# A fused linear attention and gated feed-forward kernel: batch 1's convolution moved wholly to VectorE, convolution buffers cut into one-batch units, and a new written-out order

## The chip, the cores and the metric

The kernel runs on one core of a Trainium2 chip. The metric is the device time of one launch in microseconds. A core has TensorE (matrix products, written to PSUM banks), VectorE, ScalarE and GpSimd (elementwise work), and SyncE. In the profile they are PE (PEld for its weight loads), DVE, ACT, POOL and SP. DMAs are issued by SP and POOL (and two by ACT at the start); POOL's are queue q0, SP's are q1 in the profile.

## What is computed

Eight batches, eight heads, 576 positions, head size 64, model width 512, inner width 1024, in float32; inside the kernel the operands of matrix products are bfloat16.

```python
kv = np.einsum('bhsd,bhse->bhde', k, v)
out = np.einsum('bhsd,bhde->bhse', q, kv)
rms = np.sqrt(np.mean(out * out, axis=-1, keepdims=True) + 1e-06)
x = out / rms * g_norm          # then heads are put side by side: (B, S, 512)
h = np.maximum(x @ w_in, 0.0)   # (B, S, 1024)
# conv_out: three taps along the positions, zero-padded, a weight per channel
for k in range(3):
    conv_out += conv_w[k] * hp[:, k:k + S, :]
gate = 1.0 / (1.0 + np.exp(-conv_out))
return h * gate @ w_out         # (B, S, 512)
```

## The kernel before

The kernel is a list of small operations (the functions marked `@op`) and a string, `ORDER` (L67), that is its schedule. Each token names an operation with its arguments, `@` and the buffer slots that it takes, and `:1` where the work goes to the other of VectorE and ScalarE than by default. The loop at L797 calls them in that order, and each engine then runs its own instructions in the order in which they were recorded; a dependency added at the end (L807 on) keeps it so. So `ORDER` sets the order on TensorE, VectorE, ScalarE and on both DMA queues at once. Waits between engines follow from the data and from the slots: an operation that takes a slot waits until its last user is done.

The stages of a batch b (t counts the four pairs of heads, u the two halves of them, f the eight 128-wide tiles of the inner width, e the two halves of 288 positions):

- `Lq`, `Lk`, `Lv` (L301): loads of q, k and v on POOL's queue, 576 KB each in bfloat16, into two slots for each of the three. Batch 0 comes in smaller pieces (`pre`), and batch 1 in halves. `Li` and `Lo` load the weights w_in and w_out, on the same queue.
- `kv` (L358): k times v for all pairs of heads, 12 matmuls of 96x64 tiles for each pair. `kvc` and `kvn` copy the result to SBUF; `ky` (on ScalarE or VectorE) or `kx` (a DMA on SP, L449) make the copy `kvx` with the halves exchanged.
- q has to be transposed. Batches 0 to 4 do it on TensorE (`qt0`, `qt`, L380 and L388) and copy it out (`qc0`, `qc`). Batches 5, 6 and 7 do it by DMA (`dq`, L436): two transposes each on SP's queue, from the loaded q to a slot of `qT`.
- `ot` (L430, L431) or `oq` (L464, 64x64 tiles, for batches 4 to 7): q times kv. `sq` squares it on ScalarE, `oc` copies it to SBUF.
- The norm: `on`/`nl`/`mu0` in batches 0 and 1; from batch 2 `ss` (L575) adds the squares in 128x32 tiles, `ln` takes the root, `sl` splits it in two, `sp` (L603) spreads it over the partitions in 32x128 tiles, and `mu` multiplies it in. Batch 7's factor goes through DRAM (`fw`, `fr`, L610 to L617).
- `hm` (L640; `ha`, `hb` are its halves): eight matmuls of 128x288 for the inner activation of one f. `re` is the relu that writes h.
- The convolution runs in groups c (`CONV`: group 0 is batch 0, 1 is batch 1, and 2, 3 and 4 are two batches each), for pairs j of f. On VectorE: `ta` (L699, L700; two multiplications for one f), `aa` (L706; their shifted sum) and `ab` (L712; adds the middle tap). On TensorE: `cm` (L731; six matmuls with a diagonal matrix). `sg` (L742, L745) is the sigmoid on ScalarE, `mg` (L751) multiplies it into h. Before the change f 6 and 7 of group 0 and of group 1 go by `cm`, everything else by VectorE.
- `om` (L761) multiplies with w_out, eight matmuls of 128x512 for 128 rows of a pair p of batches (in p 0 and 3 in two halves of four). `oh` (L776) does the last row tile in two halves. `ea`/`eh` copy the result out, `st`/`sh` (L795, L790) store it by DMA on SP's queue.

The convolution's buffers are two tiles, `taps0` and `taps1`, of shape [128, 2 taps, 2 f, 2 batches, 584] (L198); a one-batch group uses half of one. TensorE's matmuls use the whole 128x128 array or a part of it, its tile (the profile writes it before the moving operand's shape, as 64*64). `unread` (L427) issues matmuls whose result nobody reads.

Of the kernel before, what the change touches and what calls it, by code (L numbers as in the profile page):

```python
# [52 lines left out]
BF16 = mybir.dt.bfloat16  # L53
# [22 lines left out]
sq.1.0@4 re.0.1 qt.1.1@4 hm.0.0@2 on.1.0@6 mg.0.3 qc.1.1@3 ot.1.1@4 nl.1.0@4 re.0.0:1 sq.1.1@5 kv.1.2.2@2
kvc.1.2.2.0 ta.0.0@1 mu0.1.0 kvc.1.2.2.1 on.1.1@6 Li.2 ot.1.2@2 nl.1.1@5 ot.1.3@0 ta.0.1 sq.1.2@6 mu0.1.1 aa.0.0
unread.1@6 on.1.2@6 sq.1.3@7 ab.0.0 nl.1.2@6 mu0.1.2 on.1.3@4 nl.1.3@7 Lk.2.0@0 qt.2.0@6 sg.0.3 qt.2.1@4 mu0.1.3
ha.1.2@2 hb.1.2 qc.2.1@4 sg.0.2 qc.2.0@0 ha.1.3@0 hb.1.3 re.1.2 re.1.3 hm.1.7@4 Lv.2.0@0 hm.0.4@2 mg.0.1 Lq.3.0@1
hm.0.5@0 sg.0.1 Lk.3.0@1 Lv.3.0@1 re.1.7 sg.0.0 pl ta.1.2@0 re.0.4 ta.1.3 re.0.5 hm.1.4@4 kv.2.0.4@2 Lo.0 aa.1.1  # L80
ab.1.1 mg.0.0 sg.1.3 sg.1.2 kvc.2.0.4.0@0 hm.1.5@0 kvc.2.0.4.1 ta.0.4@1 ta.0.5 ot.2.0@2 mg.1.1 aa.0.2 hm.1.6@6
re.1.4 ot.2.2@4 re.1.5 sq.2.0@0 ta.1.4@0 ab.0.2 re.1.6 qt.3.1@0 oc.2.0:1@0 qt.3.0@6 qc.3.1@1 hm.1.1@2 ot.2.1@0
sq.2.2@1 sg.0.4 oc.2.2@1 sg.0.5 sq.2.1@2 Lo.1 Lq.4.0@0 Lq.5.0@1 qc.3.0@2 ta.1.5 ot.2.3@4 re.1.1:1 sq.2.3@3 hm.1.0@6
oc.2.1 Lk.4.0@0 Lv.4.0@0 kv.3.0.4@2 re.1.0 ss.2@3 oc.2.3 mg.0.2 ln.8@0 aa.1.2 kvc.3.0.4.0:1@1 kvc.3.0.4.1:1 ab.1.2
unread.3@0 ot.3.0@4 ta.1.0@1 ot.3.1@6 sq.3.0@4 ot.3.2@0 ta.1.1 al.x2@0 oc.3.0@2 aa.1.0 sq.3.2@5 oc.3.2@3 sq.3.1@6
om.0.3.0@2 om.0.0.0@3 oc.3.1 sl.8@0 om.0.1.0@4 ot.3.3@0 om.0.1.4 ab.1.0 om.0.3.4 sq.3.3@7 oc.3.3 sp.2.1@6,0 ss.3@5
dq.5.0@3 ea.0.1@0 mu.2.1.0 Lk.5.0@1 mu.2.1.1 om.0.0.4 ea.0.3@1 ln.1@0 sp.2.0@4,6 mu.2.0.1 mu.2.0.0 dq.5.1@0
om.0.2.0@2 Lv.5.0@1 sg.1.5 sg.1.4 qtp.4.0@0 cm.1.6@6 qc.4.0@4 mg.1.2 ea.0.0@2 hm.2.5@4 sl.1@0 hm.2.2@0 sg.1.1
om.0.2.4 re.2.5 sg.1.6@0 re.2.2 ea.0.2@3 sg.1.0 sp.3.0@6,4 cm.1.7@0 mu.3.0.1 mu.3.0.0 hm.2.4@2 hm.2.7@6 sg.1.7
sp.3.1@0,4 mg.1.0 re.2.4 mg.1.3 kv.4.0.4@2 mu.3.1.0 mu.3.1.1 re.2.7 kvn.4.0.4 ky.4.0.4.0 ky.4.0.4.1 qtp.4.1@6  # L90
hm.3.4@0 hm.3.5@4 re.3.4 oq.4.1@0 re.3.5 qc.4.1@2 ta.2.4@1 ta.2.5 oq.4.0@2 hm.2.6@6 sq.4.0@0 hm.3.3@4 oc.4.0@1
hm.3.6@2 sq.4.1@1 re.2.6 aa.2.2 Lq.7.0@0 hm.3.7@6 re.3.3 oc.4.1 hm.3.1@0 re.3.6 re.3.7 hm.3.2@6 hm.2.3@2 om.0.6.0@4
st.0.0 ab.2.2 ta.2.6@0 sg.2.5 re.3.1 re.3.2 ta.2.7 oq.4.3@6 oq.4.2@0 sg.2.4 re.2.3 kv.5.0.4@5 sq.4.2@2 Lv.7.0@0
Lk.7.0@0 om.0.6.4 om.0.5.0@2 aa.2.3 ab.2.3 Lk.6.0@1 Lv.6.0@1 kvn.5.0.4 sq.4.3@3 oc.4.2@0 mg.2.2 ky.5.0.4.0:1
ea.0.6@4 ss.4@3 dq.7.0@1 oc.4.3 ky.5.0.4.1:1 oq.5.0@0 oq.5.1@4 sq.5.0@4 ta.2.2@1 om.0.5.4 sq.5.1@5 oc.5.0:1@2
om.0.4.0@6 oc.5.1 ta.2.3 oq.5.3@0 oq.5.2@4 aa.2.1 om.0.8.0@7 ea.0.5@5 ab.2.1 sq.5.3@6 om.0.4.4 sq.5.2@7 ss.5 ln.2@0
om.0.8.4 hm.2.1@2 oc.5.2@3 ea.0.8@6 oc.5.3 re.2.1 sl.2@0 hm.2.0@4 sp.4.1@0,2 ea.0.4@7 om.0.7.0@7 re.2.0 mu.4.1.0
mu.4.1.1 sp.4.0@4,0 kv.7.0.4@6 mu.4.0.0 sg.2.2 mu.4.0.1 om.0.7.4 kvn.7.0.4:1 sg.2.3 ea.0.7@2 sp.5.0@4,2 hm.3.0@0
al.h2@1 re.3.0 kx.7.0.4.0 dq.7.1@4 mu.5.0.1 mu.5.0.0 hm.4.5@2 re.4.5 sp.5.1@6,4 hm.4.1@0 mg.2.1 mu.5.1.0 hm.4.2@2
mu.5.1.1 ta.2.0@1 sg.2.7 hm.4.0@6 hm.5.3@4 ta.2.1 re.4.1 sg.2.6 mg.2.3 kx.7.0.4.1 re.4.0 re.4.2 oq.7.0@0 re.5.3  # L100
kv.6.0.4@6 oq.7.1@4 sq.7.0@0 hm.5.2@2 oc.7.0@1 aa.2.0 Lq.6.0@1 hm.4.3@0 st.0.4 dq.6.0@2 sq.7.1@1 oc.7.1 re.5.2
hm.4.4@4 st.0.5 kvn.6.0.4:1 ab.2.0 ta.3.2@0 re.4.3 hm.5.6@0 st.0.1 ta.3.3 hm.5.4@2 hm.5.1@6 sg.2.1 sg.2.0 re.4.4
re.5.6 re.5.1 re.5.4 hm.5.0@4 oq.7.3@6 oq.7.2@0 aa.3.1 re.5.0 mg.2.0 om.1.6.0@2 om.1.3.0@3 ab.3.1 st.0.3 kx.6.0.4.0
st.0.6 ta.3.0@1 dq.6.1@3 sq.7.3@2 sq.7.2@3 ta.3.1 sg.3.3 sg.3.2 hm.5.5@4 oc.7.2@0 st.0.7 aa.3.0 ss.7@0 mg.3.1 ln.4@0
al.x3@1 ab.3.0 ta.3.4@0 ea.1.3@7 re.5.5 om.1.1.0@1 oc.7.3 ea.1.6@5 kx.6.0.4.1 om.1.0.0@0 fw.4 fr.7.0@0 ea.1.1@0
oq.6.0@2 oq.6.2@6 oq.6.3@4 om.1.8.0@1 ta.3.5 ea.1.0@1 sq.6.2@4 fr.7.1@1 oc.6.2@2 oq.6.1@6 aa.3.2 om.1.4.0@0 sq.6.0@5
sq.6.3@6 sq.6.1@7 oc.6.0@3 ss.6@2 ab.3.2 oc.6.1 ea.1.8@4 ln.3@0 ea.1.4@2 hm.4.6@6 om.1.5.0@2 oc.6.3 sl.3@0 st.1.0
mu.7.0.0 sp.6.0@4,0 mu.7.0.1 re.4.6 sg.3.5 sg.3.4 ea.1.5@1 mu.6.0.0 mu.6.0.1 om.1.2.0@6 hm.4.7@4 hm.5.7@0 mu.7.1.0
om.1.7.0@7 re.4.7 sg.3.1 re.5.7 st.0.8 sp.6.1@4,2 st.0.2 st.1.8 mg.3.2 mu.7.1.1 al.h3@0 ta.3.6@0 ea.1.2@6 ea.1.7@3
hm.7.6@0 ta.3.7 sg.3.0 hm.7.2@6 re.7.6 re.7.2 mu.6.1.0 mu.6.1.1 aa.3.3 mg.3.0 ab.3.3 hm.6.0@4 re.6.0 hm.7.1@0  # L110
hm.7.0@4 re.7.1 re.7.0 st.1.2 hm.6.1@0 hm.7.3@4 hm.6.2@6 hm.7.5@2 re.6.1 ta.4.0@1 st.1.1 st.1.7 sg.3.6 sg.3.7 ta.4.1
# [13 lines left out]
def kernel(  # L125
# [11 lines left out]
    nc = tc.nc  # L137
# [708 lines left out]
```

## Time and profile before

| what | us |
|---|---|
| median of 3 runs | 180.41 (179.9 to 182.42) |
| span of the profiled execution, first to last instruction | 177.6 |
| TensorE busy | 168.4 |
| ScalarE busy | 149.7 |
| VectorE busy | 139.5 |
| GpSimd busy | 30.8 |

The profiled execution is one of its own; its span leaves out what lies around the first and last instruction, so it is set beside the lowest of the runs, 179.9, and the median. TensorE's granted clock is 1.00 in every stretch. Matmuls overlap, so a duration of a matmul (286 ns for 128x288) is longer than its share of TensorE's time; the chain, which runs from start to start, gives the share.

### The profile page before, as it was taken

The page shows a single profiled execution, that of the slowest core. Times are in us where ns is not written, and L with a number is a line of the kernel's source. Part 1 is how long each engine was busy: PE and PEld are TensorE (multiplying, and loading weights), DVE is VectorE, ACT ScalarE, POOL GpSimd, SP SyncE. Part 2 cuts the span into 40 slices and gives each one's busy share as a digit, 9 for nine tenths or more (in the row PEclk, how much of TensorE's full clock was granted, in tenths as well). Part 3 has the DMA queues.
Part 4 walks back from the last instruction along what each step waited for, and adds up shares of the span by engine and source line. Part 5 has one row for each costly group of instructions (what it writes and reads, how often), then busy time and mean ns, then how long its engine had stood idle before and what let it go on. Part 6 is the DMA issues. An engine that isn't in the chain of part 4 may idle for free.

```text
span 177.6 us, 4060 instructions
## 1 busy us (share of the span) xinstructions
PE 168.4 (95%) x1641; PEld 101.3 (57%) x1660; DVE 139.5 (79%) x235; ACT 149.7 (84%) x233; POOL 30.8 (17%) x54
## 2 busy tenths in 40 slices
PE   6989996999999999999999999999999999999992
PEld 2545753877545677753667764444677764444541
DVE  5665669999998898999799999939999999950000
ACT  2479899999999969999999999999989987764332
POOL 7995516402600013050000000000000000000000
PEclk9999999999999999999999999999999999999999
DMA  6999999999999999999999950197040003422696
GB/s 155 188 183 197 200 204 201 205 203 206 205 204 203 198 192 139 174 203 198 160 201 179 293 128 0 53 219 263 21 160 0 4 0 143 152 82 99 258 352 219
DMA packets 36219, 29.49 MB, mean 166 GB/s; under 512 B 8528, under 2 KB 31720, under 8 KB 36200
## 3 DMA queue, kind: packets, MB, share of 16 engines
q0 software_dynamic: 21760, 15.96, 59.5%
q1 hardware_dynamic: 14400, 13.26, 28.9%
q8 instruction: 13, 0.21, 0.4%
q14 instruction: 6, 0.05, 0.1%
q10 hardware_dynamic: 40, 0.01, 0.0%
HBM read 33.70 MB, written 9.58 MB: 244 GB/s over the span
## 4 chain that ended last, share of the span: by engine, by line
PE 70%; DMA 20%; POOL 4%; ACT 2%; issue 2%; POOLq 0%; ACTq 0%
PE bank L761 33%; PE bank L640 27%; DMA v_sb<-in_v_dram 10%; DMA k_sb<-in_k_dram 7%; DMA q_sb<-in_q_dram 4%; PE bank L358 3%; PE bank L464 2%; POOL q_sb L241 1%; PE bank L603 1%; PE bank L575 1%; POOL v_sb L241 1%; POOL k_sb L241 1%; PE bank L776 1%; PE bank L731 1%; PE bank L388 1%
## 5 line engine op out<-in xcount | busy, mean ns | idle before, releaser
L640 PE MATMUL bank<-xT,w_in_sb 128*128 128x288 bf16 x496 | 64.5, 286 | 0.1
L761 PE MATMUL bank<-w_out_sb,h 128*128 128x512 bf16 x268 | 63.0, 379 | 1.1 <-issue 0.6
L640 PEld LDWEIGHTS <-w_in_sb 128*128 128x128 bf16 x496 | 47.6, 98 | 14.1 <-issue 0.5
L761 PEld LDWEIGHTS <-h 128*128 128x128 bf16 x280 | 26.3, 98 | 30.6 <-issue 1.9
L646 ACT ACTIVATE h<-bank 128x576 bf16<-128x576 f32 x61 | 37.9, 657 | 4.2 <-PE bank L640 3.9
L745 ACT ACTIVATE taps<-taps,cwn 128x1152 bf16<-128x1152 bf16 (+1 forms) x36 | 38.2, 1094 | 0.1
L341 ACT ACTIVATE row<-bank 128x512 f32<-128x512 f32 (+1 forms) x37 | 21.3, 598 | 12.3 <-PE bank L761 9.3
L751 DVE TENSOR_TENSOR h<-h,taps 128x2304 bf16<-128x2304 bf16 (+1 forms) x20 | 22.2, 1113 | 2.0 <-ACT taps L745 1.2
L706 DVE TENSOR_TENSOR taps<-taps 128x2304 bf16<-128x2304 bf16 (+1 forms) x18 | 20.9, 1160 | 0.4
L712 DVE TENSOR_TENSOR taps<-taps,h 128x2304 bf16<-128x2304 bf16 (+1 forms) x18 | 20.8, 1153 | 0.3
L699 DVE TENSOR_SCALAR taps<-h,cwn 128x1152 bf16<-128x1152 bf16 (+1 forms) x36 | 16.7, 463 | 2.5 <-ACT h L646 2.4
L493 ACT ACTIVATE sq<-bank 128x576 bf16<-128x576 f32 x28 | 17.9, 676 | 0.0
L700 DVE TENSOR_SCALAR taps<-h,cwn 128x1152 bf16<-128x1152 bf16 (+1 forms) x36 | 17.5, 487 | 0.0
L629 DVE SCALAR_TENSOR_TENSOR xT<-o,cw,bank 128x576 bf16<-128x576 f32 x20 | 15.3, 809 | 2.7 <-PE bank L603 2.5
L341 ACT ACTIVATE o<-bank 128x576 f32<-128x576 f32 x22 | 15.0, 694 | 0.0
L213 ACT ACT_TABLE_LOAD x10 | 12.8, 1283 | 2.5 <-issue 2.4
L301 POOL DMA_DIRECT2D q_sb<-in_q_dram x8 | 6.2, 772 | 31.4 <-PE bank L388 16.6
L427 PE MATMUL bank<-fill 128*128 128x512 bf16 x25 | 9.0, 480 | 1.7 <-DVE fill L228 1.5
L358 PEld LDWEIGHTS <-k_sb 96*64 96x64 bf16 x384 | 7.3, 114 | 4.0 <-issue 2.6
L358 PE MATMUL bank<-v_sb,k_sb 96*64 96x64 bf16 x384 | 8.5, 199 | 1.0 <-DMA k_sb<-in_k_dram 0.7
L301 POOL DMA_DIRECT2D k_sb<-in_k_dram x8 | 6.1, 758 | 14.4 <-PE bank L358 12.5
L562 DVE SCALAR_TENSOR_TENSOR xT<-bank,cw,root 128x576 bf16<-128x576 f32 x7 | 5.6, 815 | 1.8 <-ACT root L542 1.7
(93 smaller groups left out, 135.3 us busy)
## 6 DMA issues: line engine op xcount, KB each, us to landing
out_dram<-row SPq DMA_DIRECT2D x35, 256.0 KB, 2.8
q_sb<-in_q_dram POOLq DMA_DIRECT2D x6, 576.0 KB, 13.7
k_sb<-in_k_dram POOLq DMA_DIRECT2D x6, 576.0 KB, 14.7
v_sb<-in_v_dram POOLq DMA_DIRECT2D x6, 576.0 KB, 16.3
factor<-factor SPq DMA_DIRECT2D x4, 288.0 KB, 4.9
w_in_sb<-in_moe_w_in_dram POOLq DMA_DIRECT2D x4, 256.0 KB, 8.7
w_out_sb<-in_moe_w_out_dram POOLq DMA_DIRECT2D x2, 512.0 KB, 18.0
q_sb<-in_q_dram POOLq DMA_DIRECT2D x4, 144.0 KB, 4.6
```

Source lines behind the costliest of these rows:

```text
L341: nc.scalar.activation(to, fr, AX.Copy)
L358: nc.tensor.matmul(ps[i][i * D:(i + 1) * D, t - t0, :], k_sb[:, 2 * t + i, r * D:(r + 1) * D], v_sb[:, 2 * t + i, r * D:(r + 1) * D], star ...
L493: nc.scalar.activation(in_order(b, s), product(b, t), AX.Square)
L640: nc.tensor.matmul(ps[:, e, :HS], w_in_sb[:, t, f * P:(f + 1) * P], x[:, t, e * HS:(e + 1) * HS], start=(t == 0), stop=(t == NT - 1))
L646: nc.scalar.activation(to, fr, AX.Relu)
L699: nc.vector.tensor_scalar_mul(tap[:, 0, f % 2, :n, 8:8 + S], h[:, f], cwn[:, 0, f:f + 1])
L700: nc.vector.tensor_scalar_mul(tap[:, 1, f % 2, :n, :S], h[:, f], cwn[:, 2, f:f + 1])
L706: nc.vector.tensor_add(tap[:, 1, :, :n, :S], tap[:, 0, :, :n, 7:7 + S], tap[:, 1, :, :n, 1:1 + S])
L712: nc.vector.tensor_add(y, y, h[:, 2 * j:2 * j + 2])
L745: nc.scalar.activation(y, y, AX.Sigmoid, scale=cwn[:, 1, f:f + 1])
L751: nc.vector.tensor_mul(h, h, T["tap", c, j][:, 1, :, :n, :S])
L761: nc.tensor.matmul(T["om", p, m], h[:, f, m * P:(m + 1) * P], w_out_sb[:, f, :], start=(f == 0), stop=(f == NF - 1))
```

## The change

Three things change. Batch 1's tiles f 6 and 7 are convolved by VectorE (`ta`, `aa`, `ab`) and no longer by `cm`. The convolution's buffers become one tile of four one-batch units; a two-batch group takes two neighbouring units, seen through a rearranged view, a one-batch group takes one. And `ORDER` is written anew, by a planner that counts each change of TensorE's tile shape. The new order also chooses again which engine runs `re`, `oc`, `ea`, `kvc`, `kvn`, `ky`, `qc0` and `dg`, and the order of the loads on POOL's queue and of the transposes, kvx copies and stores on SP's.

The code outside `ORDER`:

```diff
+    def units(n):
+        s = slots.pop(0)
+        return taps[:, s:s + n].rearrange("p b k f w -> p k f b w")
...
-    taps = [consts.tile([P, 2, 2, 2, TW], BF16, name=f"taps{i}") for i in range(2)]
+    taps = consts.tile([P, 4, 2, 2, TW], BF16, name="taps")
...
-        for t in taps:
-            nc.vector.memset(t[:, 0, :, :, 7:8], 0.0)
-            nc.vector.memset(t[:, 1, :, :, S:S + 1], 0.0)
+        nc.vector.memset(taps[:, :, 0, :, 7:8], 0.0)
+        nc.vector.memset(taps[:, :, 1, :, S:S + 1], 0.0)
...
-            T["tap", c, f // 2] = taps[slots.pop(0)]
+            T["tap", c, f // 2] = units(CONV[c][1])
...
-                T["tap", c, f // 2] = taps[slots.pop(0)]
+                T["tap", c, f // 2] = units(CONV[c][1])
```

Of `ORDER`, lines with the tokens that matter to what follows: batch 1's last pair, the transposes, batch 6's and 7's loads, and the stores and kvx copies around them.

```diff
-dq.5.0@3 ea.0.1@0 mu.2.1.0 Lk.5.0@1 mu.2.1.1 om.0.0.4 ea.0.3@1 ln.1@0 sp.2.0@4,6 mu.2.0.1 mu.2.0.0 dq.5.1@0
-om.0.2.0@2 Lv.5.0@1 sg.1.5 sg.1.4 qtp.4.0@0 cm.1.6@6 qc.4.0@4 mg.1.2 ea.0.0@2 hm.2.5@4 sl.1@0 hm.2.2@0 sg.1.1
-om.0.2.4 re.2.5 sg.1.6@0 re.2.2 ea.0.2@3 sg.1.0 sp.3.0@6,4 cm.1.7@0 mu.3.0.1 mu.3.0.0 hm.2.4@2 hm.2.7@6 sg.1.7
...
-hm.3.6@2 sq.4.1@1 re.2.6 aa.2.2 Lq.7.0@0 hm.3.7@6 re.3.3 oc.4.1 hm.3.1@0 re.3.6 re.3.7 hm.3.2@6 hm.2.3@2 om.0.6.0@4
-st.0.0 ab.2.2 ta.2.6@0 sg.2.5 re.3.1 re.3.2 ta.2.7 oq.4.3@6 oq.4.2@0 sg.2.4 re.2.3 kv.5.0.4@5 sq.4.2@2 Lv.7.0@0
-Lk.7.0@0 om.0.6.4 om.0.5.0@2 aa.2.3 ab.2.3 Lk.6.0@1 Lv.6.0@1 kvn.5.0.4 sq.4.3@3 oc.4.2@0 mg.2.2 ky.5.0.4.0:1
-ea.0.6@4 ss.4@3 dq.7.0@1 oc.4.3 ky.5.0.4.1:1 oq.5.0@0 oq.5.1@4 sq.5.0@4 ta.2.2@1 om.0.5.4 sq.5.1@5 oc.5.0:1@2
...
-al.h2@1 re.3.0 kx.7.0.4.0 dq.7.1@4 mu.5.0.1 mu.5.0.0 hm.4.5@2 re.4.5 sp.5.1@6,4 hm.4.1@0 mg.2.1 mu.5.1.0 hm.4.2@2
-mu.5.1.1 ta.2.0@1 sg.2.7 hm.4.0@6 hm.5.3@4 ta.2.1 re.4.1 sg.2.6 mg.2.3 kx.7.0.4.1 re.4.0 re.4.2 oq.7.0@0 re.5.3
-kv.6.0.4@6 oq.7.1@4 sq.7.0@0 hm.5.2@2 oc.7.0@1 aa.2.0 Lq.6.0@1 hm.4.3@0 st.0.4 dq.6.0@2 sq.7.1@1 oc.7.1 re.5.2
...
+Lq.5.0@1 dq.5.0@2 ea.0.2@3 re.2.2 ab.1.1 hm.2.7@4 re.2.7 ab.1.3 sp.3.0@0,6 sg.1.1 hm.2.4@2 mu.3.0.1 mu.3.0.0
+mg.1.0 hm.2.3@4 sp.3.1@0,6 re.2.4 sg.1.2 kv.4.0.4@2 mu.3.1.0 mu.3.1.1 kvn.4.0.4:1 re.2.3 dq.5.1@0 qtp.4.1@4 qc.4.1@1
...
+ab.2.2 ta.2.6@0 re.3.3 om.0.7.0@0 oq.4.1@6 Lq.7.0@0 sg.2.5 re.3.2:1 sg.2.4 oq.5.2@2 Lq.6.0@1 sq.4.1@3 re.3.1:1
...
+oq.5.0@4 sq.5.0@6 ta.2.2@2 oq.5.1@6 om.0.7.4 oc.5.0@3 om.0.4.0@1 ss.4@3 Lk.7.0@0 dq.6.1@1 sq.5.1@7 ss.5 ln.2@0
...
+ea.0.6@6 sp.4.1@4,2 Lv.7.0@0 mu.4.1.0 mu.4.1.1 dq.7.1@0 om.0.8.4 re.2.1 sg.2.6 sp.4.0@6,4 mu.4.0.0 dq.7.0@2 kv.7.0.4@0
+mu.4.0.1 hm.3.0@2 sp.5.0@6,4 kvn.7.0.4 Lv.6.0@1 re.3.0:1 mu.5.0.1 ea.0.8@7 sg.2.7 st.0.8 mu.5.0.0 al.h2@0 hm.4.0@0
+st.0.6 hm.4.5@2 st.0.5 al.x3@0 re.4.0 re.4.5 kx.7.0.4.0 sp.5.1@0,4 sg.2.2 hm.4.1@6 re.4.1 mu.5.1.0 kx.7.0.4.1 mu.5.1.1
...
+hm.4.4@0 Lk.6.0@1 re.5.4 oq.7.1@2 oq.7.0@4 re.4.4 kv.6.0.4@6 sq.7.0@0 mg.2.1 kvn.6.0.4 sq.7.1@1 dq.6.0@3 hm.5.3@0
```

On SP's queue the order up to batch 7's products thus goes from two transposes of batch 5, a store, a transpose of batch 7, a kvx copy, the other transpose of batch 7 and a kvx copy, to two transposes of batch 5, a store, one of batch 6, two of batch 7, three stores and two kvx copies. The products `oq.7.0` and `oq.7.1` read the transpose `dq.7.0` and both kvx copies. On POOL's queue the loads for batches 6 and 7 go from q7, v7, k7, k6, v6, q6 to q7, q6, k7, v7, v6, k6. The loads ahead of w_out's are the same ones in another order; the last of them is batch 3's q in place of its v. The number of changes of TensorE's tile shape in the order (a tile of more than 64 rows or columns counted as full in that direction) goes from 80 to 73.

## The prediction, made before the changed kernel ran

> **What bounds the kernel now.** I read the page first, for who is busy, then the chain in order of time, for where the end comes from.
>
> ```profile
> span 177.6 us, 4060 instructions
> PE 168.4 (95%) x1641; PEld 101.3 (57%) x1660; DVE 139.5 (79%) x235; ACT 149.7 (84%) x233; POOL 30.8 (17%) x54
> PE 70%; DMA 20%; POOL 4%; ACT 2%; issue 2%; POOLq 0%; ACTq 0%
> ```
>
> Three engines are close to full. The chain runs over loads first (DMA 20%) and over TensorE after that. Its pieces (start, us, what):
>
> ```profile
> 28.67 17.11 DMA v_sb<-in_v_dram
> 45.78 0.14 issue
> 45.91 0.95 PE bank L358 x48
> ...
> 57.05 0.74 PE bank L731 x6
> ...
> 79.40 1.83 PE bank L761 x8
> ...
> 96.64 0.25 PE bank L464 x4
> ...
> 119.65 1.73 PE bank L761 x8
> ```
>
> Until 45.78 the load queue decides: v of batch 3 lands there, 17.11 us after its issue, because everything ahead in that queue has to land first. From 45.9 to 174.3 nearly every piece is TensorE with no gap, so whatever leaves TensorE there leaves the time. Six L731 matmuls take 0.74 us, 0.123 each. Eight L761 matmuls take 1.73 us where the next group has the same tile shape and 1.83 where it has another (at 79.40 a 64-row group follows): a change of tile shape costs 0.1 us.
>
> Next the busy time by stretch (start:end, length, then PE, PEld, DVE, ACT, POOL), to see who stands close behind TensorE:
>
> ```profile
> 50.00:60.00 10.00, 9.78 (x76) 5.27 (x75) 8.70 (x16) 9.97 (x18) 0.00 (x0) 1.00 1.32 204
> 60.00:70.00 10.00, 10.00 (x136) 7.20 (x135) 8.25 (x13) 8.00 (x15) 2.29 (x3) 1.00 1.32 175
> 70.00:80.00 10.00, 9.79 (x125) 6.19 (x126) 9.67 (x13) 10.00 (x18) 2.45 (x3) 1.00 1.30 183
> 80.00:100.00 20.00, 19.68 (x241) 12.41 (x242) 18.94 (x27) 19.94 (x30) 0.00 (x0) 1.00 1.28 197
> ```
>
> VectorE is 91% busy from 50 to 100 (45.56 of 50) and ScalarE 96%. The last column is GB/s: about 200, flat, so DMA is saturated there too. That made me look at the queues: SP's instructions and the landing times of the transposes (L436), then POOL's loads.
>
> ```profile
> 56.40 7.41 SPq L436 DMA_TRANSPOSE qT<-q_sb  x2
> 78.24 1.51 SPq L436 DMA_TRANSPOSE qT<-q_sb  x1
> 90.41 0.56 SPq L449 DMA_DIRECT2D kvx<-kvn  x1
> ```
>
> ```profile
> DMA to landing us min/median/max: 4.2/10.7/16.0
> ```
>
> ```profile
> 65.74 0.77 POOL L301 DMA_DIRECT2D q_sb<-in_q_dram  x1 [16.55 <-PE bank L388]
> 66.50 0.77 POOL L301 DMA_DIRECT2D v_sb<-in_v_dram  x1
> 67.26 0.77 POOL L301 DMA_DIRECT2D k_sb<-in_k_dram  x1
> ```
>
> A transpose lands 4.2 to 16.0 us after its issue, at best when no load runs beside it. The three loads at 65.74 are batch 7's; batch 6's k, v and q go last, from 77.14.
>
> **The change, part by part.** The sum is made on the profiled execution, 177.6 us. The median of the runs, 180.41, lies 2.8 above that span; I add 2.8 at the end.
>
> Batch 1's last pair of tiles. Off TensorE: cm.1.6 and cm.1.7, 12 matmuls at 0.123 = 1.5 us, on the path: **-1.5**. On VectorE: four multiplications (0.28 to 0.36 each), aa (0.76) and ab (0.75), 2.7 to 3.0 us. ScalarE's two sigmoids read SBUF (0.78) in place of PSUM (0.65): +0.3.
>
> Tile shapes. Counting groups in the two orders, with rows over 64 as a full tile, shape changes fall from 80 to 73, and behind the first output matmul from 49 to 45: 4 x 0.1 = **-0.4**. The other three, and two fewer filler matmuls, lie ahead of 45.8, where loads decide: 0.
>
> First output matmul. It needs w_out, whose loads stand behind the same loads as before. I take 0; bounds -0.6 (it started at 48.56, the last v landed at 45.78 and half of w_out, 0.52 MB at 204 GB/s, takes 2.6) and +1.0 (batch 3's q is now last, so transposes, two copies of 0.75 and products follow it).
>
> Moved evictions and the one-batch units. Net seven relus, five o copies and nine row copies go from ScalarE to VectorE, and some kv copies go back. At 0.67, 0.67 and 0.6, with the convolution's 2.7, less about 2 going back: VectorE +14 us, ScalarE -9. Some 3.3 of it are evictions after 160, where VectorE was idle. Ahead of that VectorE's work nears 99% of TensorE's. The cover of the moved work is TensorE's own stream, and that cover is now as thin as the difference, about 1 us. Bounds: 0, and +9 if VectorE keeps the roughly 10 us of waits that it has from 50 to 160. I take 0, as the next item gives VectorE time to catch up. Two-batch buffers become two strided pieces with the same element counts; no row shows such a shape. The nearest, 2x576 pieces, take 0.76 for 1152 and 1.36 for 2304 elements. I take 0; bounds 0 and, if a split cost as much as two instructions (2 x 0.76 against 1.36), 0.16 on each of the 36 long additions and products, 5.8, inside the +9.
>
> Queues. This is what I expect to decide. POOL's order was q7, v7, k7, k6, v6, q6; it becomes q7, q6, k7, v7, v6, k6. q6 takes the slot of batch 5's q and so waits until both transposes of batch 5 have landed; k7 and v7 now stand behind it. SP's order becomes batch 6's first transpose, then batch 7's two, then three output stores, then batch 7's kvx copies; the first product of batch 7, which was ready with room to spare, needs the third transpose and the copies. Step by step, with 0.59 MB a load, 2.9 us at 204 GB/s:
> v of the third batch lands at 45.8 as now (q of it, after the change); w_out adds 5.2 and five loads (v4, k4, q4, v5, q5) 14.5: q5 lands at 65.4, where now it lands before 56.40, when its transpose goes out.
> Its two transposes took 17.9 us now (56.40 to 58.3 + 16.0), with loads running all along. Only k5 and q7 are left to run beside them, to about 72. Bounds 73.8 (two at 4.2) and 83.3; I take 76.
> q6 goes out then. A load into an empty queue took 4.1 for a quarter of the size at the start, so about 6.3: q6 lands at 82.3, and three transposes start.
> From there four loads and three transposes (0.295 MB each) are 3.25 MB. While both kinds run, the total is 191 GB/s (60 to 67): 17.0 us, 99.3. Three stores, 0.79 MB at the 255 GB/s of 95 to 100, 3.1: batch 7 can start at **102.4**.
> TensorE would be there at 98.0: 96.64 now, less 1.5, plus three L640 groups more ahead of it (2.95), less 0.1. Wait **+4.4**. Smaller waits earlier (k7 and v7 by 89 against 87.6; batch 5's products at 75.4 against 76) are inside this one. Bounds: 0.8 (pair at 73.8, and it stays 0 if transposes outrun loads) and 11.7 (pair at 83.3).
>
> Here a rule of the Trainium skill can be set against the row. The row: transposes land 10.7 us after issue in the median. "DMA: Bandwidth & Descriptors", section "Latency and other measured facts", gives a DMA transpose 261 GB/s of effective bandwidth; by that an estimate is 1.1 us for each, batch 5's pair would land before 70, and the wait would be 0. This trace does not agree beside loads (10.7), and its best, 4.2, is latency too.
>
> Sum: 177.6 - 1.5 - 0.4 + 4.4 = 180.1; with 2.8, **182.9 us**, 1.4% over 180.41.
>
> **The rivals.**
> Transposes keep up. If the pair of batch 5 lands by 74 and the later three share better than one alone beside loads, no wait is left: 177.6 - 1.9 = 175.7, 178.5 us. For it: the 4.2. Against it: the median of 10.7 and a flat 200 GB/s. The Trainium skill's figure above is this case.
> Faster outright. The same, and the small gaps of TensorE after 50 (about 1.3 us, as in 9.78 of 10) go too, since the order was redone: 174.3, 177.1 us, and a start earlier by 0.6 would make it 176.5. Against it: VectorE has no room.
> VectorE becomes the bound (the slower side). From 48.5 to 160 it has about 101 us of work now (the table above, carried on to 160, has 99.9 of 110 from 50 on), and 111.6 after. If its waits stay at 10.1, it ends at 170.2; nine us of TensorE's last products, which need its last product, and 3.3 of tail follow: 182.5, 185.3 us. It decides once more than 3.3 us of these waits remain (TensorE's end 172.4, less 9, less 160.1), and passes 184.0 at 8.8. For it: rows such as 8.70 of 10 on TensorE's full stretches show that it does wait. Against it: with more to do it waits less.
> The queue's wait at its upper end (11.7) gives 187.4, 190.2 us.
>
> **How the numbers follow.** Wait of 2 to 7 us at batch 7: 0.46, a time from 180.5 to 185.5, about a third of it over 184.0. Transposes keep up: 0.24, 178 to 180.5. Faster outright: 0.06. VectorE the bound: 0.16, 183 to 187, most over 184.0. Upper end: 0.08. A change of 2% is about what a measurement of this kernel can tell; 2% are 176.8 and 184.0. So faster 0.06, same 0.58 (0.24 + 0.30 + 0.04), slower 0.36. The range leaves out the faster case and the upper end: 178.3 to 187.2; the likeliest case alone has 180.5 to 185.5.
>
> **What would show it.** TensorE's part: L731's successor has 12 matmuls, and L761 x8 shows 1.83 less often. The queue: POOL sits 8 us or more before q of batch 6 for the qT transposes; GB/s falls below 150 somewhere from 72 to 80; TensorE has a gap of several us before its first products of batch 7, released by a kvx or qT DMA. If that gap is under 1 us, this step is wrong. VectorE: over 150 us busy; if it were the bound, TensorE's gaps from 50 to 160 would be many, short, and released by VectorE. An end of TensorE within 0.5 us of 172.4 with no such gaps would make the forecast wrong on the good side; a late first output matmul (over 49.6) on the bad one.

## The result and the profile after

The changed kernel takes 188.21 us (median, 188.04 to 189.33), the kernel before 180.17 beside it: a ratio of 1.048, interval 1.044 to 1.052. The forecast was 182.9. Ratios here and below leave out executions that were over 1.5% above their kernel's fastest, while medians take in all of them, so the two need not match. The profiled execution took 188.11 with a span of 186.3, against 177.6 before: 8.7 us more.

The head of the page of the changed kernel (busy time, granted clock, GB/s in 40 slices of 4.66 us):

```profile
span 186.3 us, 4083 instructions
...
PE 169.5 (91%) x1646; PEld 100.5 (54%) x1646; DVE 153.4 (82%) x256; ACT 140.5 (75%) x216; POOL 31.0 (17%) x54
...
PEclk9999999999999999999999999999699999999999
...
GB/s 149 184 197 200 201 201 204 205 204 206 205 204 203 204 167 171 96 202 191 163 175 353 117 57 31 57 142 306 34 113 0 0 4 56 0 152 355 114 287 223
```

The 14 us went to VectorE and 9 left ScalarE, as worked out. The 96 GB/s at 74.5 is the pause that the forecast expected. One digit of the clock, a 6 at 130, has no counterpart before: for 3.4 us there, from 131.0 to 134.4, the granted clock was half. Such a stretch is called a dip below.

The chain of waits, from 97 us on (start, length, what):

```profile
97.70 4.83 DMA kvx<-kvn
...
117.46 1.28 ACT L216
119.28 1.76 DMA factor<-rs
...
121.83 5.32 DMA factor<-factor
...
127.97 1.24 DVE xT L631 x2
...
131.55 3.30 PE bank L763 x8
134.85 15.68 PE bank L642 x128
150.54 23.31 PE bank L763 x108
```

Before, this chain was nearly all TensorE from 45.9. Now it runs over ScalarE and VectorE from 65.2 to 78.8, and it leaves TensorE twice more from 95 on: for batch 7's copies, and for a round trip that the forecast never priced, batch 7's factor, written to memory (`fw`) and read back (`fr`). Then eight L763 products take 3.30 us, where eight took 1.83: that is the half clock.

The timeline of that place (start, length, engine, line; idle time before it and its releaser in brackets):

```profile
116.41 0.68 PE L577 MATMUL bank<-sq,sel 128*32 128x288 bf16 x16
...
117.46 1.28 ACT L216 ACT_TABLE_LOAD   x1
...
118.75 0.50 ACT L586 ACTIVATE rs<-bank,eps_sb 128x288 f32<-128x288 f32 x1
119.28 0.33 SPq L612 DMA_DIRECT2D factor<-rs  x1
...
127.24 0.82 DVE L627 SCALAR_TENSOR_TENSOR xT<-o,cw,factor 128x576 bf16<-128x576 f32 x1 [3.75 <-DMA factor<-factor]
127.97 1.53 DVE L631 SCALAR_TENSOR_TENSOR xT<-o,cw,bank 128x576 bf16<-128x576 f32 x2
128.84 0.30 PE L605 MATMUL bank<-wparts,spread 32*128 32x288 bf16 x4 [1.69 <-DVE xT L631]
```

The same steps in the kernel before:

```profile
109.68 1.28 ACT L213 ACT_TABLE_LOAD   x1
109.81 0.43 PE L575 MATMUL bank<-sq,sel 128*32 128x288 bf16 x8
...
110.98 0.50 ACT L584 ACTIVATE rs<-bank,eps_sb 128x288 f32<-128x288 f32 x1
111.50 0.33 SPq L610 DMA_DIRECT2D factor<-rs  x1
...
120.90 1.54 DVE L625 SCALAR_TENSOR_TENSOR xT<-o,cw,factor 128x576 bf16<-128x576 f32 x2
```

In both orders `mu.7.0.0` (L627, L625 before) stands ahead of batch 6's scalings on VectorE. Before, its factor went out at 111.5 and was there by 120.9. Now `ln.4` (L586) comes 7.8 us later. Most of that, 6.6, is the sum that it reads: `ss.7` (L577) starts at 116.41 in place of 109.81, next to `ss.6`. The rest is ScalarE's table load (L216), which stands behind a sigmoid here and ran while `ss.7` did before. So the factor lands at 127.1, VectorE stands idle for 3.75 us in front of it, and batch 6's scalings (L631), whose data is ready, stand behind it. TensorE waits for the banks that they read.

The first products of batch 7, with SyncE's instructions ahead of them:

```profile
95.56 1.50 SPq L797 DMA_DIRECT2D out_dram<-row  x3
97.10 1.32 SPq L451 DMA_DIRECT2D kvx<-kvn  x2
...
101.17 0.31 PE L466 MATMUL bank<-qT,kvn 64*64 64x288 bf16 x1
102.58 0.31 PE L466 MATMUL bank<-qT,kvx 64*64 64x288 bf16 x2 [1.10 <-DMA kvx<-kvn]
```

The first that reads a copy (`kvx`) starts at 102.58, against 102.4 in the forecast. But TensorE is there only at 101.17, not at 98.0. It had waited earlier, most of it at 76 to 79 (the lines show VectorE's wait for a copy by ScalarE, GpSimd's wait for batch 5's transposes, then TensorE's two waits for VectorE):

```profile
74.54 0.42 DVE L345 CAST kvx<-bank 64x256 bf16<-64x256 f32 x1 [1.58 <-ACT kvx L343]
...
75.37 0.77 POOL L303 DMA_DIRECT2D q_sb<-in_q_dram  x1 [7.60 <-DMA qT<-q_sb]
...
78.11 0.28 PE L466 MATMUL bank<-qT,kvn 64*64 64x288 bf16 x1 [1.16 <-DVE h L650]
...
78.78 0.28 PE L466 MATMUL bank<-qT,kvn 64*64 64x288 bf16 x1 [0.35 <-DVE h L650]
```

So VectorE, too, stood idle for 1.58 us shortly before TensorE's waits, for a copy that ScalarE, busy without a pause from 65.6 to 75.2, made at 74.1.

The 8.7 us, by the starts of TensorE's products less what the work takes: first output matmul 49.58 against 48.56, +1.0; TensorE's work behind it -1.9; waits at 67.8 and 70.6 (ScalarE's relus) +0.8, at 76 to 79 +1.85, at 101 +1.3, at 126.9 to 131.5 +3.45 (1.85, 0.58, 1.02); half clock from 131.0 to 134.4, +1.5; from the last product to the end 4.7 against 3.3, +1.4. Together 9.4; the kernel before has small gaps of its own behind 48.56, about 0.6, that are to be taken off. The -1.9 is the forecast's own figure; the counts of products and of shape changes in the two traces (45 against 49) bear it out.

### The profile page after: what moved, and what is told of

It is laid out like the page before. It is cut to its first block, busy times and chain, and to the rows that moved or that the text cites. A ratio compares the mean times of both kernels' runs of the same rounds, so it can differ in the third digit from the quotient of the medians.

```text
span 186.3 us, 4083 instructions
## 1 busy us (share of the span) xinstructions
PE 169.5 (91%) x1646; PEld 100.5 (54%) x1646; DVE 153.4 (82%) x256; ACT 140.5 (75%) x216; POOL 31.0 (17%) x54
## 4 chain that ended last, share of the span: by engine, by line
PE 58%; ACT 13%; DMA 11%; DVE 6%; issue 4%; POOL 4%; SPq 1%; POOLq 0%; ACTq 0%; DVEq 0%
PE bank L763 28%; PE bank L642 20%; DMA w_in_sb<-in_moe_w_in_dram 5%; ACT h L648 3%; ACT sq L495 3%; DMA factor<-factor 3%; DMA kvx<-kvn 3%; PE bank L360 2%; ACT taps L747 2%; PE bank L466 1%; ACT L216 1%; ACT o L343 1%; POOL q_sb L244 1%; DVE xT L631 1%; PE bank L382 1%
## 5 line engine op out<-in xcount | busy, mean ns | idle before, releaser
L763 PE MATMUL bank<-w_out_sb,h 128*128 128x512 bf16 x280 | 64.9, 385 | 0.9 <-DVE xT L631 0.9
L763 PEld LDWEIGHTS <-h 128*128 128x128 bf16 x280 | 26.9, 99 | 33.2 <-issue 3.8
L747 ACT ACTIVATE taps<-taps,cwn 128x1152 bf16<-128x1152 bf16 (+1 forms) x38 | 39.9, 1077 | 5.6 <-DVE taps L714 5.5
L648 ACT ACTIVATE h<-bank 128x576 bf16<-128x576 f32 x54 | 34.0, 654 | 4.8 <-PE bank L642 4.5
L343 ACT ACTIVATE row<-bank 128x512 f32<-128x512 f32 (+1 forms) x28 | 15.8, 598 | 19.5 <-PE bank L763 17.7
L701 DVE TENSOR_SCALAR taps<-h,cwn 128x1152 bf16<-128x1152 bf16 (+1 forms) x38 | 17.5, 460 | 0.5 <-ACT h L648 0.5
L702 DVE TENSOR_SCALAR taps<-h,cwn 128x1152 bf16<-128x1152 bf16 (+1 forms) x38 | 17.9, 470 | 0.0
L631 DVE SCALAR_TENSOR_TENSOR xT<-o,cw,bank 128x576 bf16<-128x576 f32 x20 | 15.3, 808 | 0.4 <-PE bank L605 0.4
L343 ACT ACTIVATE o<-bank 128x576 f32<-128x576 f32 x17 | 11.4, 676 | 0.0
L650 DVE TENSOR_SCALAR h<-bank 128x576 bf16<-128x576 f32 x10 | 7.5, 753 | 3.3 <-PE bank L642 3.3
L345 DVE COPY row<-bank 128x512 f32<-128x512 f32 (+1 forms) x9 | 5.9, 659 | 4.7 <-PE bank L763 3.7
L429 PE MATMUL bank<-fill 128*128 128x512 bf16 x25 | 8.3, 457 | 1.5 <-DVE fill L231 1.5
```

What stands on the lines that cost most here:

```text
L343: nc.scalar.activation(to, fr, AX.Copy)
L648: nc.scalar.activation(to, fr, AX.Relu)
L747: nc.scalar.activation(y, y, AX.Sigmoid, scale=cwn[:, 1, f:f + 1])
L763: nc.tensor.matmul(T["om", p, m], h[:, f, m * P:(m + 1) * P], w_out_sb[:, f, :], start=(f == 0), stop=(f == NF - 1))
```

## The experiments

The theory: the loss comes from four or five places in the new order, batch 7's factor the largest. Rival 1: VectorE, now nearly as full as TensorE up to 160, is the bound. Rival 2: the buffers cost. Later, how the waits add up came to be the question. Runs of one changed version lie up to 8 us apart, and the mean granted clocks of such runs go from 0.968 to 1.0; so I read waits from traces beside the medians. A trace is of one execution. The length of a wait in the text is from one product's start to the next, less what the first takes; the brackets in the lines are a little shorter.

### The parts alone, in the kernel before

Buffers alone (`b_units`): one tile of four units, tokens on slot 1 take unit 2.

> The kernel before with the buffers alone: one tile of four one-batch units, the two old buffers being units 0-1 and 2-3, in the old order. Theory: 180.2 us, within 0.7. Rival 2 (the buffers themselves cost, by the strided layout or by waits on the shared tile): 181.5 us or more, with longer VectorE operations on the buffers than 0.51, 1.36 and 1.37 us.

179.71 us, ratio 0.999 (0.996 to 1.002). The long sums and products of this kernel:

```profile
L708 DVE TENSOR_TENSOR taps<-taps 128x2304 bf16<-128x2304 bf16 x12 | 16.3, 1362 | 0.3
L714 DVE TENSOR_TENSOR taps<-taps,h 128x2304 bf16<-128x2304 bf16 x12 | 16.2, 1353 | 0.2
```

They took 1362 and 1354 ns before: the unit layout costs nothing that shows, and rival 2 falls.

Convolution alone, three places (`b_conv`, `b_conv2`, `b_conv3`):

```diff
-cm.1.6@6 ... cm.1.7@0
+first:  mg.1.2 ta.1.6@0 ta.1.7 aa.1.3 ab.1.3
+second: mu.3.0.0 ta.1.6@0 ta.1.7 ... mu.3.1.1 aa.1.3 ab.1.3 ... re.3.5 mg.1.3
+third:  mu.3.0.0 ta.1.6@0 ta.1.7 ... qc.4.1@2 aa.1.3 ab.1.3 ... oc.4.1 sg.1.6 sg.1.7 ... ab.2.2 mg.1.3
```

> The kernel before with one part of the change alone: f 6 and 7 of batch 1's convolution go from TensorE (12 products of 0.123 us) to VectorE, in the old order, with the old buffers. Theory (the new order costs the 8 us, the move itself nothing): 178.5 to 180.5 us. Rival 1 (VectorE's added 4 us stands in the way of its evictions wherever it is put): 181.5 us or more.

> The kernel before with f 6 and 7 of batch 1's convolution on VectorE, as in the first try, but the seven added or moved VectorE operations stand behind the scalings of batch 3 and not ahead of the split of its factor. In the first try they stood ahead of that split: TensorE waited 2.9 us there, and the granted clock was 0.5 for the next 3.4 us. Theory (the move costs by its place in VectorE's order, not by its work): neither the wait nor the dip, 178 to 180.5 us. Rival 1 (VectorE's added work costs wherever it is): 181.5 us or more, with the wait at another place.

> The kernel before with f 6 and 7 of batch 1's convolution on VectorE, third place: the taps behind batch 3's first two scalings, the two sums behind the copy of batch 4's second q pair, sigmoids and product later still. In the two tries before, the added VectorE work stood ahead of a split (TensorE waited 2.9 us) or of that copy (2.6 us), and the clock fell to 0.5 behind each. Theory: no wait over 1 us, no dip, 178.3 to 180.5 us. Rival 1 (at 55 to 72 us the old order leaves VectorE no room for 3 more us): 182 us or more.

183.81 (1.019, 1.012 to 1.026), 183.91 (1.024, 1.021 to 1.026) and 180.69 us (1.003, 1.000 to 1.006). In the first, the split of batch 3's factor stood behind the new work:

```profile
63.32 0.43 PE L602 MATMUL bank<-wparts,spread 32*128 32x288 bf16 x4 [2.75 <-DVE wparts L593]
```

In the second a copy of q stood behind it (2.6 us), and the clock fell to half for 3.4 us behind each; in the third there is a wait of 1.2 us for ScalarE at 73.6 and no dip. My expectation was too good each time. TensorE no longer does 1.5 us of products, and in the old order the same stretch gives them back as waits: the move pays in none of the three places, and costs 2% in the two where it stands ahead of something that TensorE needs.

Queue order alone (`b_queue`):

```diff
-Lq.7.0@0 ... Lv.7.0 Lk.7.0 Lk.6.0 Lv.6.0 ... Lq.6.0@1
+Lq.7.0@0 Lq.6.0@1 ... Lv.7.0 Lk.7.0 Lk.6.0 Lv.6.0
-dq.7.0@1 ... kx.7.0.4.0 dq.7.1@4 ... kx.7.0.4.1 ... st.0.4 ... st.0.5 ... st.0.1 ... dq.6.1@3
+dq.6.1@1 ... dq.7.0@3 ... dq.7.1@4 ... st.0.4 st.0.5 st.0.1 kx.7.0.4.0 kx.7.0.4.1
```

> The kernel before with the changed queue order for batches 6 and 7 alone: q of batch 6 is loaded right behind q of batch 7, its first transpose goes ahead of batch 7's two, three stores stand ahead of batch 7's two small copies. TensorE is at batch 7's first products at 98.0 us here. The forecast as it stood, and the theory of stacked waits: batch 7's copies land at 101 to 103, a wait of 3 to 4.5 us there, and with the half clock that may follow a wait of that length 183 to 186.5 us. Rival (the queue order never cost more than the 1.3 us seen): at most 181.5 us.

186.66 us, 1.038 (1.032 to 1.044).

```profile
94.92 1.51 SPq L794 DMA_DIRECT2D out_dram<-row  x3
96.53 1.32 SPq L448 DMA_DIRECT2D kvx<-kvn  x2
97.33 0.31 PE L463 MATMUL bank<-qT,kvn 64*64 64x288 bf16 x1
...
101.88 0.45 PE L463 MATMUL bank<-qT,kvx 64*64 64x288 bf16 x2 [4.24 <-DMA kvx<-kvn]
```

TensorE is in time, and the wait is 4.4 us beyond the pitch of the products, the forecast's figure. With 1.1 us for batch 6's k at 88.9 and a dip from 101.9 to 105.3, worth about 1.5, that makes 7.0, beside 6.7 between the medians.

### The changed kernel, one part put right

Batch 7's factor (`a_mu7`):

```diff
-mu.7.0.0 ea.1.3@7 hm.5.7@0 mu.6.1.1 ... mu.6.0.1 sg.3.4 mu.7.1.1 ... mu.6.0.0 aa.3.0 mu.7.0.1 al.h3@1 mu.7.1.0
+ea.1.3@7 hm.5.7@0 mu.6.1.1 ... mu.6.0.1 sg.3.4 ... mu.6.0.0 mu.7.0.0 mu.7.0.1 aa.3.0 mu.7.1.0 mu.7.1.1 al.h3@1
```

> The changed kernel with batch 7's four scalings on VectorE moved behind batch 6's, so that the 3.75 us for which VectorE waits for the factor no longer holds up batch 6's scalings. Theory (this wait makes 3.45 us of TensorE's gaps from 126.8 to 131.5 and lets the granted clock fall to 0.5 from 131.0 to 134.4, worth 1.5 more): 183 to 185.5 us, and a granted clock of 1.0 after 131. Rival 1 (VectorE, 99% as busy as TensorE, is the bound): the wait shows up at the next place, 187 us or more.

184.44 us, 1.030 (1.022 to 1.038), 3.8 less.

The clock by slice, on its page, and the timeline at batch 7's factor:

```profile
PEclk9999999999999999978999999999999999999999
```

```profile
127.58 0.30 PE L605 MATMUL bank<-wparts,spread 32*128 32x288 bf16 x4
...
128.00 1.54 DVE L631 SCALAR_TENSOR_TENSOR xT<-o,cw,bank 128x576 bf16<-128x576 f32 x2 [0.24 <-PE bank L605]
...
129.46 1.54 DVE L627 SCALAR_TENSOR_TENSOR xT<-o,cw,factor 128x576 bf16<-128x576 f32 x2
```

No wait is left there, and VectorE does the same work (153.6 us against 153.4): the place of four tokens in the order, not VectorE's load, made the 3.45 us. Half my expectation of the clock failed: it is full at 131, but dips at 79.7, behind the waits at 76 to 79.

The clock alone (`a_fill`):

```diff
-mu.6.1.1 sp.6.0@4,6
+mu.6.1.1 unread.8@7 sp.6.0@4,6
```

> The changed kernel with eight products of 0.216 us that nothing reads, put on TensorE into its wait of 1.85 us ahead of batch 6's second pair of factors; every wait for work stays as it is, TensorE is only busy during it. Theory (the half clock of 3.4 us behind this wait is set by TensorE's idle time in the window of 3.4 us before it: 1.59 us or more in all that dipped, 1.58 or less in all that did not): no half clock after 131 us, and 186.3 to 187 us. Rival (the clock falls for another reason, or costs nothing): the half clock stays, 188 us or more.

186.61 us, 1.036 (1.028 to 1.044), 1.6 less, with products that nothing reads in place of a wait (clock by slice; timeline):

```profile
PEclk9999999999999999999999999999999999999999
```

```profile
126.55 1.89 PE L429 MATMUL bank<-fill 128*128 128x512 bf16 x8
```

The data wait is as long as it was (VectorE 4.13 us for the factor), and in this execution, 185.69, the dip is gone. Its price of about 1.5 is read from the products (3.30 us in place of 1.83). The medians can't give it: the other three executions have a mean granted clock of 0.99, as the changed kernel's four do, so the clock fell somewhere in them too, and one of them took 185.52.

SyncE's order (`a_kx`), and GpSimd's with it (`a_queue`):

```diff
-dq.6.1@1 ... dq.7.1@0 dq.7.0@2 ... st.0.8 st.0.6 st.0.5 kx.7.0.4.0 kx.7.0.4.1 ... dq.6.0@3
+dq.7.1@0 dq.7.0@2 ... kx.7.0.4.0 kx.7.0.4.1 st.0.8 st.0.6 st.0.5 ... dq.6.1@1 dq.6.0@3
 a_queue also:
-Lq.7.0@0 Lq.6.0@1 ... Lk.6.0@1
+Lq.7.0@0 ... Lk.6.0@1 Lq.6.0@1
```

> The changed kernel with SyncE's order alone put right: the transpose of batch 6 behind the two of batch 7, and the three stores behind batch 7's two small copies; the loads keep the changed order. Theory: batch 7's copies land at 94 to 98 us in place of 102.5, the wait of 1.28 us goes, 186.5 to 187.5 us. Rival (the queue is worth the 4.4 us of the forecast): 183.5 to 184.5 us.

> The changed kernel with the queue order undone for batches 6 and 7: q of batch 6 is loaded last, its transpose pair stands behind batch 7's, and the three stores stand behind batch 7's two small copies. Theory (TensorE is 3 us late when it gets there, so the queue shows as 1.3 us only): 186.3 to 187.3 us. Rival, the forecast as it stood (the queue costs 4.4 us): 183.5 to 184.5 us.

187.8 (1.043, 1.038 to 1.047) and 188.52 us (1.039, 1.034 to 1.045). In both the wait of 1.28 is gone, and by the medians little or nothing is gained. The profiled execution of `a_kx`, with one dip as in the changed kernel, took 186.47 against 188.11, 1.6 less, and its last product starts 1.3 sooner; the other three have mean granted clocks of 0.974 to 0.977, lower than any of the changed kernel's. So the medians alone do not show that this wait is worth little. In `a_queue` another wait comes: with loads running on behind q of batch 7, batch 5's second transpose lands at 80.0 in place of 74.8, and TensorE waits 3.3 us for it. The late q of batch 6, which the forecast saw only as a harm, had kept loads away from that transpose.

The waits at 76 to 79 (`a_mid`, `a_mid2`):

```diff
 a_mid:
-kvn.5.0.4 ky.5.0.4.0 ... ab.2.2 ta.2.6@0 re.3.3 ... sg.2.5 re.3.2:1 sg.2.4 ... re.3.1:1
+kvn.5.0.4:1 ky.5.0.4.0:1 ... re.3.2:1 re.3.1:1 ab.2.2 ta.2.6@0 re.3.3 ... sg.2.5 sg.2.4
 a_mid2:
-sg.2.5 re.3.2:1 sg.2.4 ... re.3.1:1
+re.3.2 re.3.1 sg.2.5 sg.2.4
```

> The changed kernel with the evictions at 71 to 79 us put right alone: the two copies of batch 5's k-by-v products go from ScalarE to VectorE, and VectorE's two evictions of batch 3's first product go ahead of batch 2's taps. Takes away the 1.85 us that TensorE waits at 76.7 to 78.8. Theory (stacked waits: what is gained here is lost again at 101, where the queue sets when batch 7's products may start): the wait of 1.28 us for batch 7's copies grows to some 3, and the time stays within 0.8 of 188.2 us. Rival (each wait is worth its own length): 186 to 186.6 us.

> The changed kernel with one edit at 71 to 79 us: VectorE's two evictions of batch 3's first product, behind the taps there, go to ScalarE, into the 1.26 us for which ScalarE waits for those taps. The first try at this stretch delayed ScalarE's sigmoids and put a wait of 3.4 us behind them in place of the 1.85. Theory (stacked waits): the 1.85 us at 76.7 to 78.8 go, the wait for batch 7's copies at 101 grows from 1.28 to some 3, and the time stays within 0.8 of 188.2 us. Rival (each wait is worth its own length): 186 to 186.6 us.

189.66 us (1.055, 1.049 to 1.061), and 184.92 to 192.62 in four runs, too far apart to compare. Neither settles what the 1.85 is worth: the first made a wait of 3.4 us for ScalarE's copies up to 82.7, the second one of 1.64 up to 80.6, in place of the 1.85.

VectorE's added work (`a_noconv`; it leaves out VectorE's six operations for f 6 and 7 of batch 1, and the sigmoids read what lies in the buffer):

```diff
 def ta(c, f):
     tap = T["tap", c, f // 2]
+    if (c, f // 2) == (1, 3): return
-aa.1.3 ... ab.1.3
```

> The changed kernel without VectorE's six operations for f 6 and 7 of batch 1's convolution (four taps and two sums, some 3.0 us at 45 to 60): that part is left out, and its sigmoids read what lies in the buffer. Theory (VectorE's added work is covered; the new order's own places make the waits): the waits of 1.85 us at 76 to 79 stay, 187 to 188.5 us, at most 0.9 less by the later start. Rival 1 (VectorE is the bound and its lag is carried on): those waits shrink below 0.6 and the time falls by 1.5 us or more, to 186.7 or less.

187.41 us, 1.039 (1.034 to 1.044), 0.8 less.

```profile
78.23 0.28 PE L466 MATMUL bank<-qT,kvn 64*64 64x288 bf16 x1 [0.97 <-DVE h L650]
...
78.89 0.28 PE L466 MATMUL bank<-qT,kvn 64*64 64x288 bf16 x1 [0.35 <-DVE h L650]
```

With 3 us less on VectorE the waits are 1.15 and 0.53, beside 1.33 and 0.52, and the wait for the factor stays (2.25 us at L605). With `a_mu7`, and with VectorE idle for 1.58 us ahead of the waits at 76 to 79 in the changed kernel, this is against rival 1.

The end (`a_tail`):

```diff
-st.1.4 ... st.1.1 ... st.1.3 ... st.1.5 ... st.1.8
+st.1.4 st.1.1 st.1.3 st.1.5 st.1.8 ...
```

> The changed kernel with four stores of the second output pair, whose rows have long been ready, moved from the last 50 us of SyncE's order to the place where it has nothing else to store. Theory (at the end nine stores stand in one queue, and the last lands 4.6 us after the last product against 3.3 before): the end comes 0.5 to 1.3 us sooner, 187 to 187.8 us. Rival (the last nine stores are all rows that only just became ready, so older ones don't matter): 188.2 within 0.5.

186.89 us, 1.038 (1.034 to 1.041). The end itself did not move in the profiled execution (189.81, the longest of the six): 4.6 us from the last product to the end, and the last store lands 3.15 us after its issue, against 3.16. Three of the six runs had a mean granted clock of 0.998 or more, which the changed kernel's had not, so the lower time is not shown to come from the stores. In the changed kernel the stores at the end are these:

```profile
178.36 3.79 SPq L797 DMA_DIRECT2D out_dram<-row  x7
...
182.25 0.57 SPq L792 DMA_DIRECT2D out_dram<-row  x1
```

Seven whole rows go out in the 3.9 us ahead of the last half row, where the kernel before has four and a half in as long (from 171.0 to 174.7). Moving four older stores didn't change that. Another order of the last products was not tried, so the cause of the longer end stays open.

### Parts put right together

`a_all`: `a_mu7`, `a_mid` and `a_kx`. `a_all2`: with `a_mid2` in place of `a_mid`. `a_best`: with a third edit of that stretch, and `a_tail`. `a_late_queue`: `a_best` without `a_kx`. The third edit:

```diff
-re.3.3 ... sg.2.5 re.3.2:1 sg.2.4 oq.5.2@2 ... sq.4.1@3 re.3.1:1 sq.5.2@4 oc.5.2@2 ... om.0.5.4 mg.2.2 oc.5.3 oc.4.1 ea.0.5@2 ... oq.5.1@6 om.0.7.4
+re.3.3 re.3.2 re.3.1 ... oq.5.2@2 ... sq.5.2@4 oc.5.2@2 sg.2.5 ... aa.2.3 ... om.0.5.4 ab.2.3 oc.5.3 sq.4.1@3 oc.4.1 ea.0.5@2 sg.2.4 mg.2.2 ... om.0.7.4 oq.5.1@6
```

> The changed kernel with the three corrections together: batch 7's scalings behind batch 6's, the evictions at 71 to 79 us, and SyncE's order. Theory (three waits of 3.45, 1.85 and 1.28 us, and a clock dip that needs a long wait ahead of it and is worth 1.5 to 1.7): 188.2 - 8.1 = 180.1, within 1, and a granted clock of 1.0 from 10 us to the last product. Rival 1 (VectorE is the bound): 184 us or more, with waits for VectorE that have moved.

> The changed kernel with three corrections: batch 7's scalings behind batch 6's, the two evictions on ScalarE, and SyncE's order (batch 6's first transpose behind batch 7's, the three stores behind batch 7's copies). Theory: 188.2 less 3.45, 1.85, 1.28 and 1.5 for the dip of the clock, 180.1 us within 1, no half clock between 10 us and the last product. What is then left against the kernel before is the later start (1.2) and the stores at the end (1.3), less the 1.9 us of TensorE's work. Rival 1 (VectorE is the bound): 184 us or more.

> The changed kernel with all corrections: batch 7's scalings behind batch 6's; SyncE's order; a new attempt at 71 to 79 us (two evictions to ScalarE, its two sigmoids of batch 2 behind the squares and copies that free TensorE's banks, VectorE's sums of the next taps ahead of the product that waits for those sigmoids, and four products ahead of the last small ones of batch 5); the four stores moved up. Theory: 182.05 of the second version with three corrections, less its one wait of 1.64 us and up to 1 at the end, 179.5 to 180.7 us. Rival 1 (VectorE or ScalarE has no room there): 181.5 us or more, with the wait at a third place.

> The kernel with all corrections, but with SyncE's order as the change has it: batch 6's transpose ahead of batch 7's two, three stores ahead of batch 7's copies. Theory (with TensorE in time the queue shows in full; copies at 102.5, TensorE there at 99.3 in place of 101.2): a wait of 3 to 3.4 us for the copies, and 2.8 to 4.5 us more than the kernel with all corrections. The forecast as it stood: 4.4 us more. Rival (the queue never cost more than 1.3 us): at most 1.5 us more.

`a_all`: 185.68 us (1.034, 1.031 to 1.037), with the 3.4 us wait of `a_mid` and a dip behind it. `a_all2`: four executions, 182.05, 182.06, 186.83 and 187.94, with mean granted clocks of 0.997, 1.0, 0.984 and 0.978, too far apart to compare as one. The profiled one is the first, with no dip before the last product and one long wait left:

```profile
80.46 1.89 PE L763 MATMUL bank<-w_out_sb,h 128*128 128x512 bf16 x8 [1.48 <-ACT o L343]
```

From 188.1 to 182.05 is 6.1, where 3.45, 1.28, 1.5 and the 0.2 between 1.85 and 1.64 make 6.4: in an execution without a dip, the waits for the factor and the copies, and the dip, are worth about their lengths. `a_best`: 183.24 us (1.019, 1.015 to 1.022). The third edit took away the wait at 80 and put 2.4 us at 83 to 91, for ScalarE's squares and the split behind them. ScalarE there (the column behind VectorE's 7.73):

```profile
80.00:90.00 10.00, 8.76 (x66) 4.02 (x64) 7.73 (x12) 9.95 (x17) 0.00 (x0) 1.00 1.30 184
```

So three edits moved this wait on, and the third found ScalarE with nothing free. Whether some order of this stretch has no wait is open. No changed version beat the kernel before. `a_late_queue`: 184.57 us (1.024, 1.020 to 1.029), 1.3 more than `a_best`, a wait of 0.8 for the copies: my 3 us were wrong, as TensorE again came only at 101.9. `b_queue` is the run that answers what the queue costs a TensorE in time.

## Why the prediction was wrong

The steps of the queue came out: q of batch 5 landed at 65.05 (forecast 65.4), batch 5's pair at 74.79 (76), q of batch 6 at 81.28 (82.3), the third transpose at 99.11 (99.3), batch 7's first product with a copy began at 102.58 (102.4). Of its signs, the rate fell to 96 GB/s and VectorE is over 150 us busy; GpSimd stood 7.6 us before q of batch 6, for 8 or more, and the gap ahead of batch 7 was 1.28, not several. The first rival has transposes that keep up with loads. Batch 5's took 4.1 and 8.1 us for 0.295 MB each in the changed kernel, and the second took 12.4 where loads ran beside it (`a_queue`). The Trainium skill's 261 GB/s in "DMA: Bandwidth & Descriptors" ("Latency and other measured facts") is not what these transposes get.

TensorE's work: 1.9 us less, as summed. VectorE's added work at 0: right about the load as far as `a_mu7` and `a_noconv` show it, but the orders of ScalarE and VectorE that came with it were not free, 0.8 and 1.85. The first output matmul came 1.0 later, the upper bound, not 0. The queue's +4.4: right as a price (`b_queue`, 4.42), and here it showed as 1.28, since 3.2 us of it were used up by TensorE's lateness. Up to 102 us the sum is right to 0.2 us, though two of its terms were too small and one too large, because the time at which batch 7's copies land is set by DMAs: they land at 102.5 here, and at 101.8 in `b_queue` with TensorE in time, and what TensorE lost before that comes off its wait for them.

The step that failed is the sum behind that: "Sum: 177.6 - 1.5 - 0.4 + 4.4 = 180.1" lets everything behind batch 7's first product run as before. It did not look at what ScalarE and VectorE do next with batch 7. Span 186.3 less 180.1 is 6.2; factor 3.45, half clock 1.5, end 1.4 make 6.35. That `fw.4` goes out late could be read from the order: `ss.7` and `ln.4` now stand beside `ss.6` and `ln.3`, and `mu.7.0.0` still ahead of `mu.6`. I had priced each moved eviction, but not what is queued behind an instruction that waits for a DMA. For the end the sum had no term. The 2.8 added for the median was too much: here the median lies 1.9 above the profiled span, so the forecast of 182.9 missed by 5.3 and not by 6.2.

Three figures beside the sum don't follow from their terms: with the pair of transposes at 73.8 in place of 76, the lower bound of the wait is 2.2, not 0.8; the lower bound of the first output matmul is -0.2 (45.78 and 2.6 against 48.56), not -0.6; and ScalarE's -9 is nearer -11 by the counts given, though 9.2 was measured. None of them changes the forecast.

Of the rivals, the queue's wait at its upper end gave the nearest time, 190.2 beside 188.2, by luck: the wait that it puts at 11.7 us was 1.28. The rival "VectorE becomes the bound" gave 185.3, and its sign, gaps released by VectorE, did appear: 5.3 of the 7.4 us have that releaser. Its mechanism is not what happened in the largest of them: VectorE itself stood idle for the factor there, and with its work unchanged the wait goes.

## What to carry to other kernels

A wait for data whose landing is set by DMAs takes in the delays of the waiting engine ahead of it. Repairing the transfer alone then gains only what is left of its cost (here a wait of 1.28 us, where the price is 4.4), so that cost has to be measured where the engine comes in time. That repairing the delays alone gains little follows from the same argument and was not shown. In a hand-written order, look at every instruction that waits for a DMA, and at what is queued behind it with its data ready. Where the engines stand near 80% busy or more, as here, try a move alone in the old order first, at more than one place: in this kernel its place decided between no change and 2% more.

## What the runs showed of the hardware

The granted clock falls to half for 3.41 us behind a window of 3.41 us in which TensorE stood idle for part only. Counting windows from the clock's first change in each trace, that begin between 20 and 172 us: eleven windows with 1.97 to 3.38 us idle were all followed by half clock; of four with 1.58 to 1.65 two were; none with 1.51 or less was. The 3.3 us wait of `a_queue` fell across two windows, 1.51 and 1.58, and cost no clock; a 2.75 us wait with 2.51 us idle in one window did (`b_conv`). So where a wait falls in the window decides. That the same kernel can have the dip in one execution and not in the next fits the mean granted clocks of `a_all2` (1.0 to 0.978), but only one execution of each kernel has a trace.

The Trainium skill, "TensorE: Matmul & The Clock Gate", section "What's actually happening", has a free-running window of 3413 ns, and an idle window as what halves the clock; the length agrees. Its section "Why this matters for your kernels" asks for no gaps over some 3 us; here gaps of 1.85, 0.58 and 1.02 us, of which 1.97 us fell into one window, were enough.

Transposes beside loads are slow: batch 5's second transpose took 8.1 us in the changed kernel, with q of batch 7 loading beside it and the next load held, and 12.4 in `a_queue`, with loads going on.
